# The low part of relu in two of eight token groups: from one VectorE instruction to a ScalarE and a GpSimd instruction

## The chip, the cores and the metric

The kernel runs on one core of a Trainium2 chip. The metric is device microseconds of one execution. The engines are TensorE (PE: matmuls; PEld: its weight loads), VectorE (DVE), ScalarE (ACT), GpSimd (POOL) and SyncE (SP), whose queue issues the DMAs used here. Each engine executes its own list of instructions in a fixed order and waits on semaphores for the others.

## What is computed

Three stages follow each other: a recurrence over 768 tokens (32 batch-heads of width 40), a feed-forward block with a norm, and a second feed-forward block with a three-tap convolution and a gate. Only the second stage is touched by the change:

```python
xn = (x - mu) / np.sqrt(var + 1e-06) * g_ln
ch = np.maximum(xn @ w_ch1, 0.0) @ w_ch2
return (x + ch).astype(np.float32)
```

`x` has 4 x 768 rows of 320; `w_ch1` is 320 x 1280, `w_ch2` is 1280 x 320. The weights arrive as float64.

## The kernel before

The first half of the program (to about 490 us) is the recurrence. Then come eight groups of 384 tokens (TG). Each goes through `ffn` (the first block, ten column blocks f = 0..9 of 128 hidden units) and `hidden` (the second block's up-product, eight blocks, results in the tile `h`), while convolution, gate and down-product of finished pieces run as tasks beside them.

**Two parts for every number.** Products are made in a rounded format (FP32R), and precision is kept by splitting each operand into a high part (the rounded value) and a low part (value minus high part). Three matmul passes (high x high, high x low, low x high) replace one. So the relu between the two products is also needed in two parts, `rh` and `rl`. `relu_parts` (lines 973 to 979) makes `rh` on ScalarE from the PSUM tile `ups` (L977) and `rl = max(ups, 0) - rh` on VectorE in one instruction, again from PSUM (L978).

**The work of one block f.** TensorE makes `ups` with 8 matmuls (L960, `up`) and adds the block into three PSUM tiles `acc` with 9 matmuls (L970, `down`): six that read `rh`, three that read `rl`. `ffn` calls `up` one block ahead of `down`. There are two PSUM buffers for `ups` and three buffers each of `rh` and `rl`. After block 9, VectorE adds `acc` to `x` (L995), which frees the three PSUM tiles for the next transposes (`tps`, L938).

**Weights are converted beside the first two groups.** In groups 0 and 1, and in the `hidden` blocks that follow, the float64 weights still come in. One conversion (`Weights.load`, `value`, `step`) is: a DMA into one of four buffers (`raw`, twice, and two halves of `o`; L792); ScalarE squares the high words into `q` (L803); VectorE builds the float32 value `v` in four dependent instructions (L804, L805, L807, L810); ScalarE rounds it to the high part, for instance `w4h` (L818, CAST); GpSimd subtracts for the low part, `w4l` (L820). There are two buffers of `v`. From the start of group 0 there are 6 conversions left for w2 (128x320), 12 for w3 (128x256), 8 for w4 (128x320) and one small one for the convolution's taps.

**Order.** The order of each engine's list is not written by hand: the program is emitted in the order of `first`, `ffn` and `hidden`, and a list scheduler with its own timing model then sorts the instructions of each engine. On the chip the order is fixed. Of importance here: an instruction of ScalarE that waits for a conversion (L818) holds up the relus behind it.

Of the kernel before, what the change touches and what calls it, by code (L numbers as in the profile page):

```python
# [10 lines left out]
AF = mybir.ActivationFunctionType  # L11
ALU = mybir.AluOpType
# [718 lines left out]
N1, N2 = F1 // 128, F2 // 128  # L731
TG = 384
# [98 lines left out]
class Mlp:  # L831
# [138 lines left out]
                self.mm = self.nc.tensor.matmul(acc[n][:, 0:DM], lhsT=l, rhs=r, start=(f == 0 and i == 0),  # L970
                                                stop=(f == nf - 1 and i == 2)).ins

    def relu_parts(self, ps):
        nc = self.nc
        rh = self.pr.tile([128, TG], F32R, tag="rh", name="rh")
        rl = self.pr.tile([128, TG], F32R, tag="rl", name="rl")
        nc.scalar.activation(rh, ps, AF.Relu)  # L977
        nc.vector.scalar_tensor_tensor(out=rl, in0=ps, scalar=0.0, in1=rh, op0=ALU.max, op1=ALU.subtract)  # L978
        return rh, rl

    def ffn(self, g, xt, mid):

        nc = self.nc
        acc = [self.psa.tile([128, 512], F32, tag="a", name="acc") for _ in range(NT)]
        self.ws.until(1)
        parts = self.relu_parts(self.up(self.w1h, self.w1l, 0, xt))
        for f in range(N1):
            self.ws.until(f + 2)
            nxt = self.relu_parts(self.up(self.w1h, self.w1l, f + 1, xt)) if f + 1 < N1 else None
            self.down(acc, parts, self.w2h, self.w2l, f, N1)  # L990
            parts = nxt
            mid(f)
        x = self.x2[g]
        for n in range(NT):
            nc.vector.tensor_tensor(out=x[:, n], in0=acc[n][:, 0:DM], in1=x[:, n], op=ALU.add)  # L995
        return x
# [295 lines left out]
```

## Time and profile before

| | us |
|---|---|
| median of 3 runs | 933.29 (930.16 to 936.09) |
| the profiled execution | 932.86 |
| its span, first to last instruction | 931.1 |

| engine | busy, us | share of the span |
|---|---|---|
| PE | 810.3 | 87% |
| DVE | 650.7 | 70% |
| ACT | 511.7 | 55% |
| POOL | 297.5 | 32% |

The shares are averages over very different stages. In the page's forty slices TensorE is at 8 to 9 tenths from 490 us on, VectorE at 9 from about 490 to 610 us and far lower later, and GpSimd does little after 570 us. What a change in groups 0 and 1 is worth must be read from about 498 to 590 us.

### The profile page before, as it was taken

The numbers are of one execution on the slowest core, as the hardware profiler recorded it, in microseconds if no ns is written. First come the engines' busy times: TensorE is split into PE (matmuls) and PEld (weight loads), VectorE is DVE, ScalarE is ACT, GpSimd is POOL, SyncE is SP. The second block draws the span as 40 slices with busy tenths as digits, with TensorE's granted clock in tenths as the row PEclk, the third lists the DMA queues.
The fourth block names the chain that finished last, engine by engine and source line by source line (L and its number), as shares of the span: only waits on it lengthen the run. The fifth ranks groups of instructions, "written<-read, shape, count | busy, mean of one in ns | idle before, by whom it ended". The sixth has DMA issues, their size and how long they took to land.

```text
span 931.1 us, 24745 instructions
## 1 busy us (share of the span) xinstructions
PE 810.3 (87%) x9911; PEld 714.8 (77%) x9911; DVE 650.7 (70%) x1528; ACT 511.7 (55%) x1166; POOL 297.5 (32%) x519
## 2 busy tenths in 40 slices
PE   1655579899879989979788898999999999999995
PEld 1444368667657767767667797999999999999994
DVE  8859757666656855787898999957368563847264
ACT  6257448677558656556454346836256353727263
POOL 9415269368359276086112222000000000000014
PEclk9766679999999989989899899999999999999998
DMA  6994696667687774773746341001010100000000
GB/s 165 202 239 122 184 211 135 153 130 186 160 170 175 180 149 123 137 158 85 176 120 171 86 128 48 15 1 36 1 50 1 36 1 15 15 1 29 1 15 32
DMA packets 218543, 94.20 MB, mean 101 GB/s; under 512 B 176860, under 2 KB 207924, under 8 KB 218420
## 3 DMA queue, kind: packets, MB, share of 16 engines
q1 hardware_dynamic: 217524, 90.24, 40.9%
q0 software_dynamic: 896, 2.30, 1.2%
q8 instruction: 80, 1.31, 0.6%
q14 instruction: 43, 0.35, 0.1%
HBM read 63.78 MB, written 28.72 MB: 99 GB/s over the span
## 4 chain that ended last, share of the span: by engine, by line
PE 45%; DVE 23%; DMA 10%; ACT 7%; SPq 5%; issue 4%; POOL 4%; DVEq 0%; ACTq 0%; POOLq 0%
PE ups L960 17%; PE acc L970 8%; PE accb L970 8%; DVE r L495 5%; PE reps L478 2%; PE tps L938 2%; SPq L448 2%; SPq L217 2%; PE aps L396 2%; DMA raw<-in_moe_w_ch_dram 2%; PE tr L322 2%; DVE l L414 2%; ACT yt L134 2%; PE xrps L547 1%; DMA ld_w<-in_w_dram 1%
## 5 line engine op out<-in xcount | busy, mean ns | idle before, releaser
L1024 POOL TENSOR_TENSOR pl<-c,ph 128x512 fp32r<-128x512 f32 x8 | 13.5, 1708 | 334.2 <-ACT ph L1021 334.2
L978 DVE SCALAR_TENSOR_TENSOR rl<-ups,rh 128x384 fp32r<-128x384 f32 x80 | 44.2, 554 | 83.0 <-ACT rh L977 82.9
L977 ACT ACTIVATE rh<-ups 128x384 fp32r<-128x384 f32 x80 | 38.9, 488 | 101.8 <-PE ups L960 101.6
L495 DVE TENSOR_TENSOR r<-zhps,zmask 32x576 f32<-32x576 f32 x96 | 72.0, 750 | 25.8 <-PE zhps L491 24.0
L435 POOL TENSOR_TENSOR sv<-sv,svt 128x30 f32<-128x30 f32 (+9 forms) x150 | 80.9, 539 | 10.0
L433 POOL TENSOR_TENSOR svt<-sv 128x30 f32<-128x30 f32 (+9 forms) x150 | 78.7, 525 | 9.6
L960 PE MATMUL ups<-xh,w1h 128*128 128x384 f32 x240 | 81.5, 342 | 0.0
L960 PE MATMUL ups<-xh,w1l 128*128 128x384 f32 x240 | 81.0, 337 | 0.0
L970 PE MATMUL acc<-w2h,rh 128*128 128x320 f32 x240 | 71.6, 310 | 1.6 <-ACT rh L977 1.6
L508 PE MATMUL xps<-r,l 128*40 128x72 f32 x1536 | 61.8, 238 | 11.1 <-issue 6.7
L970 PE MATMUL acc<-w2l,rh 128*128 128x320 f32 x240 | 71.4, 307 | 0.0
L508 PEld LDWEIGHTS xps<-r,l 128*40 128x40 f32 x1536 | 54.6, 124 | 18.0 <-issue 8.9
L960 PE MATMUL ups<-xh,w3h 128*128 128x384 f32 x192 | 64.3, 339 | 2.0 <-ACT h L1002 2.0
L134 ACT COPY yt<-xps 40x256 f32<-40x256 f32 x96 | 35.2, 367 | 55.5 <-DVE r L519 52.4
L960 PE MATMUL ups<-xh,w3l 128*128 128x384 f32 x192 | 64.6, 336 | 0.0
L414 DVE TENSOR_TENSOR l<-aps,mask 32x256 f32<-32x256 f32 x96 | 40.0, 417 | 29.4 <-ACT pst L401 28.2
L970 PE MATMUL accb<-w4h,ph 128*128 128x320 f32 x192 | 59.0, 314 | 1.2 <-ACT ph L1021 1.2
L970 PE MATMUL accb<-w4l,ph 128*128 128x320 f32 x192 | 58.6, 308 | 0.0
L960 PE MATMUL ups<-xl,w1h 128*128 128x384 f32 x160 | 54.2, 339 | 0.4 <-DVE xl L944 0.4
L1013 DVE SCALAR_TENSOR_TENSOR c<-h,taps,c 128x256 f32<-128x256 f32 (+1 forms) x88 | 45.7, 528 | 12.6 <-ACT c L1011 12.4
L970 PE MATMUL accb<-w4h,pl 128*128 128x320 f32 x192 | 53.4, 311 | 0.8 <-POOL pl L1024 0.7
L519 DVE TENSOR_TENSOR r<-xps,ge 40x320 f32<-40x320 f32 x96 | 46.8, 488 | 9.4 <-PE xps L508 8.0
(190 smaller groups left out, 2278.6 us busy)
## 6 DMA issues: line engine op xcount, KB each, us to landing
l<-ks SPq DMA_DIRECT2D x44, 160.0 KB, 3.6
raw<-in_moe_w_ch_dram SPq DMA_DIRECT2D x17, 320.0 KB, 3.4
ks<-p_b SPq DMA_DIRECT2D x12, 416.0 KB, 3.3
ks<-p_k SPq DMA_DIRECT2D x12, 416.0 KB, 4.3
ld_w<-in_w_dram SPq DMA_DIRECT2D x24, 160.0 KB, 3.4
ld_k<-in_k_dram SPq DMA_DIRECT2D x24, 160.0 KB, 4.4
ld_a<-in_a_dram SPq DMA_DIRECT2D x24, 160.0 KB, 3.4
ld_b<-in_b_dram SPq DMA_DIRECT2D x24, 160.0 KB, 4.4
```

The lines of the kernel that those rows point to most:

```text
L134: return self.nc.scalar.copy(out, in_).ins
L414: nc.vector.tensor_tensor(out=lv[v0:v0 + C, :, :, y, c, 32 * half:32 * half + C], in0=pv[64 * y:64 * y + C, :, :, half], in1=self.mask[64 ...
L433: eng.tensor_tensor(out=tmp, in0=sv[:, 0:u, u:u + 1].to_broadcast([128, u, m]), in1=sv[:, u:u + 1, u + 1:C].to_broadcast([128, u, m]), op= ...
L435: last = eng.tensor_tensor(out=sv[:, 0:u, u + 1:C], in0=sv[:, 0:u, u + 1:C], in1=tmp, op=ALU.add)
L495: nc.vector.tensor_tensor(out=r1[z0:z0 + 32, :, :, MO[y]:MO[y] + 72], in0=ps[32 * y:32 * y + 32], in1=self.zmask[32 * y:32 * y + 32].rearr ...
L508: nc.tensor.matmul(ps[x0:x0 + D, j >> 2, o:o + 72], lhsT=l2[:, i, :], rhs=r1[:, j, MO[y]:MO[y] + 72], start=True, stop=True)
L519: last = nc.vector.tensor_tensor(out=r2[X0:X0 + D, :, :, VO[y]:VO[y] + D], in0=pv[x0:x0 + D, :, :, v:v + D], in1=ge[X0:X0 + D, :, :, y, c: ...
L960: self.mm = self.nc.tensor.matmul(ps, lhsT=l, rhs=r, start=(i == 0), stop=(i == len(passes) - 1)).ins
L970: self.mm = self.nc.tensor.matmul(acc[n][:, 0:DM], lhsT=l, rhs=r, start=(f == 0 and i == 0), stop=(f == nf - 1 and i == 2)).ins
L977: nc.scalar.activation(rh, ps, AF.Relu)
L978: nc.vector.scalar_tensor_tensor(out=rl, in0=ps, scalar=0.0, in1=rh, op0=ALU.max, op1=ALU.subtract)
L1013: nc.vector.scalar_tensor_tensor(out=c, in0=h(1), scalar=w(1), in1=c, op0=ALU.mult, op1=ALU.add)
```

## The change

In groups 0 and 1 (`g < 2`) `relu_parts` gets a scratch tile `r`, a slice of the tile `h` that `hidden` fills later. ScalarE then makes relu twice from the same PSUM tile, once rounded into `rh` and once in full into `r` (L979 of the changed kernel), and GpSimd subtracts, `rl = r - rh` (L980). Groups 2 to 7 keep the VectorE instruction (now L982). Lines below are six higher than before from there on, so L995 becomes L1001 and L1002 becomes L1008.

```diff
-    def relu_parts(self, ps):
+    def relu_parts(self, ps, r=None):
         nc = self.nc
         rh = self.pr.tile([128, TG], F32R, tag="rh", name="rh")
         rl = self.pr.tile([128, TG], F32R, tag="rl", name="rl")
         nc.scalar.activation(rh, ps, AF.Relu)
-        nc.vector.scalar_tensor_tensor(out=rl, in0=ps, scalar=0.0, in1=rh, op0=ALU.max, op1=ALU.subtract)
+        if r is not None:
+            nc.scalar.activation(r, ps, AF.Relu)
+            nc.gpsimd.tensor_tensor(out=rl, in0=r, in1=rh, op=ALU.subtract)
+        else:
+            nc.vector.scalar_tensor_tensor(out=rl, in0=ps, scalar=0.0, in1=rh, op0=ALU.max, op1=ALU.subtract)
         return rh, rl
 
     def ffn(self, g, xt, mid):
...
+        r = lambda f: self.h[:, f % N2, 1:TG + 1] if g < 2 else None
         self.ws.until(1)
-        parts = self.relu_parts(self.up(self.w1h, self.w1l, 0, xt))
+        parts = self.relu_parts(self.up(self.w1h, self.w1l, 0, xt), r(0))
         for f in range(N1):
             self.ws.until(f + 2)
-            nxt = self.relu_parts(self.up(self.w1h, self.w1l, f + 1, xt)) if f + 1 < N1 else None
+            nxt = self.relu_parts(self.up(self.w1h, self.w1l, f + 1, xt), r(f + 1)) if f + 1 < N1 else None
```

The scheduler sorts the whole stage anew. Three places matter.

ScalarE, end of group 1, before: `rh_8322` is block 8 of the group, `rh_8355` block 9; each CAST is the end of one w4 conversion.

```order
L818 CAST w4h_7579<-v_8271 128x320
L803 ACTIVATE q_8336<-o_7653 128x320
L977 ACTIVATE rh_8258<-ups_8249 128x384
L818 CAST w4h_7579<-v_8303 128x320
L803 ACTIVATE q_8369<-raw_8344 128x320
L977 ACTIVATE rh_8290<-ups_8281 128x384
L818 CAST w4h_7579<-v_8335 128x320
L803 ACTIVATE q_8389<-raw_8377 128x320
L977 ACTIVATE rh_8322<-ups_8313 128x384
L818 CAST w4h_7579<-v_8368 128x320
L803 ACTIVATE q_8434<-o_7653 128x320
L977 ACTIVATE rh_8355<-ups_8346 128x384
```

The same place of the changed kernel, from the third w4 CAST on: `rh_8307` is block 7, `rh_8340` block 8, `rh_8374` block 9, and the rows `h_7584<-ups` the second relus.

```order
L818 CAST w4h_7579<-v_8354 128x320
L803 ACTIVATE q_8409<-raw_8397 128x320
L977 ACTIVATE rh_8307<-ups_8298 128x384
L979 ACTIVATE h_7584<-ups_8298 128x384
L818 CAST w4h_7579<-v_8388 128x320
L803 ACTIVATE q_8454<-o_7653 128x320
L818 CAST w4h_7579<-v_8408 128x320
L803 ACTIVATE q_8474<-o_7653 128x320
L977 ACTIVATE rh_8340<-ups_8331 128x384
L979 ACTIVATE h_7584<-ups_8331 128x384
L818 CAST w4h_7579<-v_8453 128x320
```

Block 8's relu stood behind the third w4 CAST and now stands behind the fifth; block 9's moved from behind the fourth to behind the sixth.

GpSimd, same place, changed kernel (before, the eight w4l rows follow each other with nothing between):

```order
L820 TENSOR_TENSOR w4l_7580<-v_8354,w4h_7579 128x320
L980 TENSOR_TENSOR rl_8308<-h_7584,rh_8307 128x384
L820 TENSOR_TENSOR w4l_7580<-v_8388,w4h_7579 128x320
L820 TENSOR_TENSOR w4l_7580<-v_8408,w4h_7579 128x320
L980 TENSOR_TENSOR rl_8341<-h_7584,rh_8340 128x384
L820 TENSOR_TENSOR w4l_7580<-v_8453,w4h_7579 128x320
L980 TENSOR_TENSOR rl_8375<-h_7584,rh_8374 128x384
```

Each low part now waits its turn behind the low parts of the weights.

TensorE, end of group 1 in the changed kernel, from the last matmuls of block 9's `up` on (`w1`), through block 8's six `rh` matmuls, whose rows begin here:

```order
L970 MATMUL acc<-w2h,rl 128x320 x3
L970 MATMUL acc<-w2h,rh 128x320
L970 MATMUL acc<-w2l,rh 128x320
L970 MATMUL acc<-w2h,rh 128x320
L970 MATMUL acc<-w2l,rh 128x320
L970 MATMUL acc<-w2h,rh 128x320
L970 MATMUL acc<-w2l,rh 128x320
L960 MATMUL ups<-xh,w3h 128x384
```

These are block 8's `rl` and block 9's `rh`; the first of the `hidden` blocks (8 matmuls with w3) stands ahead of them and the second behind, then block 9's `rl`. Before, block 8's `rl` followed its `rh` at once. A low part is thus wanted one block of matmuls later than before.

## Rows read from the trace of the kernel before

**Rows 1.** Busy by stretch: PE, PEld, DVE, ACT, POOL; then PEclk, DMA, GB/s
```profile
498.00:525.00 27.00, 25.05 (x156) 24.14 (x157) 24.80 (x85) 11.28 (x28) 7.82 (x8) 1.00 0.62 166
525.00:529.60 4.60, 1.35 (x9) 0.83 (x7) 4.60 (x19) 0.74 (x2) 1.03 (x1) 0.88 0.35 94
529.60:537.70 8.10, 7.85 (x35) 6.52 (x35) 7.97 (x20) 4.81 (x12) 1.47 (x2) 0.65 0.14 44
590.00:870.00 280.00, 278.92 (x1775) 277.07 (x1774) 177.57 (x468) 143.96 (x361) 0.00 (x0) 1.00 0.05 17
```
**Rows 2.** PE's waits, 498 to 600 us: in total, times, longest
```profile
PE acc L970 <- DVE rl L978: 3.1, 5, 1.6
PE ups L960 <- ACT h L1002: 2.0, 4, 1.2
PE tps L938 <- DVE x L995: 1.7, 1, 1.7
```
**Rows 3.** DVE by line and form, 500 to 566 us: count, busy us, mean ns
```profile
L978 DVE SCALAR_TENSOR_TENSOR rl<-ups,rh 128x384 fp32r<-128x384 f32 x20 | 10.8, 546 | 0.2 <-ACT rh L977 0.2
L810 DVE SCALAR_TENSOR_TENSOR v<-q,v 128x320 f32<-128x320 bf16 x10 | 6.0, 598 | 0.1
...
L922 DVE SCALAR_TENSOR_TENSOR y<-t,y 128x3 f32<-128x3 f32 x12 | 3.8, 315 | 0.0
L805 DVE SCALAR_TENSOR_TENSOR v<-raw,v 128x320 int32<-128x320 int32 x5 | 3.0, 603 | 0.0
...
L920 DVE SCALAR_TENSOR_TENSOR t<-y 128x3 f32<-128x3 f32 x12 | 2.8, 234 | 0.0
...
L921 DVE TENSOR_TENSOR t<-t,v 128x3 f32<-128x3 f32 x12 | 1.8, 149 | 0.0
```
**Rows 4.** DVE in order of time, 559 to 566 us: start, us
```profile
559.43 1.06 DVE L810 SCALAR_TENSOR_TENSOR v<-q,v 128x320 f32<-128x320 bf16 x1
560.41 0.55 DVE L978 SCALAR_TENSOR_TENSOR rl<-ups,rh 128x384 fp32r<-128x384 f32 x1
560.88 0.31 DVE L804 TENSOR_SCALAR v<-raw 128x320 int32<-128x320 int32 x1
561.22 1.07 DVE L805 SCALAR_TENSOR_TENSOR v<-raw,v 128x320 int32<-128x320 int32 x1
...
562.97 0.48 DVE L810 SCALAR_TENSOR_TENSOR v<-q,v 128x320 f32<-128x320 bf16 x1
```
**Rows 5.** POOL in order of time, from 559 us
```profile
559.03 1.10 POOL L820 TENSOR_TENSOR w4l<-v,w4h 128x320 fp32r<-128x320 f32 x1 [2.55 <-ACT w4h L818]
```
**Rows 6.** POOL by line and form, 490 to 566 us
```profile
L820 POOL TENSOR_TENSOR w3l<-v,w3h 128x256 fp32r<-128x256 f32 x12 | 10.2, 848 | 28.5 <-ACT w3h L818 28.4
L820 POOL TENSOR_TENSOR w2l<-v,w2h 128x320 fp32r<-128x320 f32 x6 | 6.1, 1027 | 15.8 <-ACT w2h L818 15.8
L820 POOL TENSOR_TENSOR w4l<-v,w4h 128x320 fp32r<-128x320 f32 x5 | 4.9, 983 | 8.6 <-ACT w4h L818 8.6
```
**Rows 7.** ACT in order of time, 558 to 566 us: third, fifth, sixth w4 cast
```profile
558.50 0.46 ACT L818 CAST w4h<-v 128x320 fp32r<-128x320 f32 x1 [2.20 <-DVE v L810]
...
559.27 0.47 ACT L977 ACTIVATE rh<-ups 128x384 fp32r<-128x384 f32 x1
...
563.49 0.46 ACT L818 CAST w4h<-v 128x320 fp32r<-128x320 f32 x1 [1.72 <-DVE v L810]
...
565.81 0.46 ACT L818 CAST w4h<-v 128x320 fp32r<-128x320 f32 x1 [1.47 <-DVE v L810]
```
**Rows 8.** PE in order of time, 560 to 565 us: block 8, last of block 9, hidden
```profile
560.19 0.30 PE L970 MATMUL acc<-w2h,rh 128*128 128x320 f32 x1
...
561.55 0.34 PE L960 MATMUL ups<-xh,w3h 128*128 128x384 f32 x1
...
564.38 0.71 PE L970 MATMUL acc<-w2h,rl 128*128 128x320 f32 x3 [0.37 <-DVE rl L978]
564.92 0.34 PE L960 MATMUL ups<-xh,w3h 128*128 128x384 f32 x1
```

## Prediction

> **What bounds the kernel now.** I read the busy times by stretch first [rows 1]. From 590 to 870 us TensorE is busy 278.92 of 280 us at full clock: whatever it is early or late by at 590 us goes straight into the end. So the change is worth what it does to TensorE between 498 and 590 us. There VectorE is the crowded engine: 24.80 of 27 us between 498 and 525 us, 4.60 of 4.60 us in the next stretch [rows 1]. ScalarE (11.28 of 27) and GpSimd (7.82 of 27) have room.
>
> The waits of TensorE come next [rows 2]. It lost 3.1 us for `rl` (L978) and 1.7 us for the sums of x (L995), both ended by VectorE, and 2.0 us for ScalarE's `h` in the `hidden` blocks. The gap at 525 to 529.6 us, where it was busy 1.35 us, is followed by 8.1 us at a mean granted clock of 0.65 (so part at 1.2, part at 2.4 GHz); that is 8.1 x 0.35 = 2.8 us more [rows 1]. All that VectorE costs TensorE here is therefore 3.1 + 1.7 + 2.8 = 7.6 us, and no relief of VectorE alone brings more.
>
> **What the change removes.** Twenty `rl` instructions of 0.546 us leave VectorE [rows 3]. They overlap their successors a little: from the start of one at 560.41 to the next instruction at 560.88 are 0.47 us [rows 4]. So 20 x 0.47 = 9.4 us of VectorE's time go, and the 3.1 us of waits for L978 with them, if nothing takes their place.
>
> **What it adds on ScalarE.** Twenty second relus. I cost them like the first ones, 0.47 us as at 559.27 [rows 7], 9.4 us in all. They lie in ScalarE's idle time (15.7 us idle of 27 between 498 and 525 us [rows 1]), and the next block's matmuls hide the later release of the PSUM buffer: one block of `hidden` matmuls and the three passes of `down` beside it are over 2 us (561.55 to 564.38 [rows 8]). Without that cover each would cost 0.47 us. I take nothing.
>
> **What it adds on GpSimd.** Twenty subtractions of 128x384. The trace has the same form, two SBUF inputs and a rounded output, at 128x256 (0.848 us) and 128x320 (0.983 to 1.027 us) [rows 6]. From 0.848 and 0.983, 0.135 us per 64 columns, my estimate at 384 is 1.12 us. With one weight subtraction per block, GpSimd needs 1.0 + 1.1 = 2.1 us, and TensorE needs 564.92 - 561.55 - 0.37 = 3.0 us for one up-product and one `down` [rows 8]. That fits. The order also wants each low part one block of matmuls later than before, so waits for `rl` should vanish. I take nothing for GpSimd's own length.
>
> **The toll on VectorE.** This is the term that decides. At 559.43 L810 takes 1.06 us; at 562.97 the same instruction takes 0.48 us [rows 4]. The long one coincides with a GpSimd subtraction that runs from 559.03 for 1.10 us [rows 5], and the L805 at 561.22 (1.07 us) looks the same. The `rl` at 560.41 is not stretched: its 0.55 us is the mean of all twenty [rows 3, 4]. So a GpSimd subtraction holds up VectorE instructions, and the one instruction that the change removes is of a kind that it does not hold up. One toll is 1.06 - 0.48 = 0.58 us. A lower bound is the mean: over L810 (10 x (0.598 - 0.48)), L805 (5 x (0.603 - 0.48)), L922 (12 x (0.315 - 0.149)) and L920 (12 x (0.234 - 0.149), the 0.149 from L921) VectorE lost 1.2 + 0.6 + 2.0 + 1.0 = 4.8 us [rows 3]. Spread over 23 subtractions [rows 6] that is 0.21 us each, with the other forms left out. An upper bound is the subtraction's whole length, 1.12 us. I take a toll of L = 0.5 us: nearer to the single 0.58, since no `rl` is left on VectorE to fill the time, less a little for norm instructions that might. Then twenty tolls are 10 us against 9.4 us saved: VectorE is not relieved at all.
>
> The Trainium skill (SBUF — State Buffer, section "Who interferes with whom") says that a VectorE instruction with two SBUF inputs and a GpSimd instruction that reads SBUF share a read interface, and that the second to start waits for the whole of the first; one with a single SBUF input goes through. The trace agrees on which instructions are stretched (L810, not `rl`), but the stretch of 0.58 us is shorter than the GpSimd instruction's 1.10 us. By that rule taken at its word the toll would be the whole 1.12 us, which is the last rival below.
>
> **What moves on ScalarE.** The scheduler placed the relus as if VectorE had become faster. Block 8's relu in group 1 stood behind the third w4 CAST and now stands behind the fifth; block 9's behind the sixth instead of the fourth. ScalarE runs in order, so these relus wait for VectorE's conversions, and TensorE waits for them, with the last of group 1 and the `hidden` blocks queued behind.
>
> Where is the fifth CAST? At 563.49 before [rows 7]. Ahead of its L810 in VectorE's list 19 `rl` and one L804 (about 0.2 us) are gone: 19 x 0.47 + 0.2 = 9.1 us; otherwise the list holds the same instructions up to there. Eighteen GpSimd subtractions are new: 18 L. With L = 0.5 the CAST comes 9.0 - 9.1 = -0.1 us off, at 563.4. From CAST to end of relu takes (559.27 + 0.47) - 558.50 = 1.24 us in the same sequence CAST, square, relu [rows 7], so the relu ends at 564.6 and TensorE can start at about 564.7. Before, it started block 8's `down` at 560.19 [rows 8]. **That is 4.5 us later.**
>
> Block 9's relu waits for the sixth CAST, at 565.81 before, again shifted by about nothing, and ends at 567.0. TensorE comes to it after six matmuls, a `hidden` block and three matmuls, 0.9 + 1.4 + 0.45 us after 564.7, at 567.5: no second wait. Block 8's `rl` follows the fifth w4l: 564.0 + 1.0 + 1.1 = 566.1, wanted at 567.0, so it is covered by 0.9 us and costs the excess if GpSimd is slower. The 0.37 us wait for `rl` at 564.38 [rows 8] goes.
>
> Group 0 has the same pattern, one conversion instead of two, and the sums of x come when VectorE comes to them. Whatever is won or lost there up to 4 us does not count: TensorE would wait at the fifth CAST for the rest.
>
> **Sum.** +4.5 - 0.37 = +4.1 us at 565 us. Of the 2.0 us waits for `h` [rows 2], which hang on ScalarE and VectorE and come at the same time while TensorE comes later, I give back two thirds, -1.3 us (an estimate). Net +2.8 us on the profiled execution's 932.86: 935.7. The median shown (933.29) is 0.4 us above that execution, so I predict 936.0.
>
> **Rivals.**
> *Tie.* The toll is about 0.3 us, near the mean. The fifth CAST comes 18 x 0.3 - 9.1 = -3.7 us earlier, the wait shrinks from 4.5 to 0.8 us, less 0.37 and part of the 1.3: 932 to 933. For it: the mean. Against: the mean includes subtractions that met an `rl`.
> *Gain.* The toll is below 0.26 us (18 L - 9.1 = -4.5, where the wait is gone). Then VectorE's waits go too, at most 7.6 us: 925. For it: GpSimd instructions may fall on norm work or idle time. Against: VectorE idles hardly at all.
> *Slower.* VectorE stands still for the subtraction's whole 1.12 us. The fifth CAST moves by 18 x 1.12 - 9.1 = +11.1 us; 11.1 + 4.1 - 1.3 = +13.9, so 947. It passes +1% (9.3 us) from L = 0.87 on. For it: the subtraction is longer than any of the stretch, and a crowded VectorE always has a two-input instruction ready. Against: 0.58 us at 1.10 us length.
>
> **How the numbers follow.** Forecast (L from 0.38 to 0.7; 933.5 to 939.5): 0.50. Tie: 0.20. Gain (924 to 930): 0.15. Slower (940 to 947): 0.15. The range leaves out the better half of the gain and most of the slow case: 927 to 943. About 1%, 9.3 us, is what a measurement can tell from no change. Faster by more than that needs more than the 7.6 us of VectorE's waits: 0.04. Slower by more: 0.11. Within: 0.85.
>
> **What would show it.** In the changed kernel's profile: L805, L807 and L810 stretched about twice as often; VectorE as busy from 498 to 566 us as before although twenty instructions are gone; a TensorE wait of about 4 us ended by ScalarE's `rh` just before the first `hidden` block, with the w4 CAST ahead of it waiting for L810; no waits for `rl` beyond 1 us. The prediction is wrong if the fifth w4 CAST comes before 560 us or after 570 us, if TensorE waits for GpSimd's `rl` instead, or if the `hidden` waits swallow the whole delay.

## The result, and the profile after

The changed kernel takes 939.24 us in the median (933.73 to 949.3, 12 runs), the kernel before 935.77 us (927.99 to 944.89) on the same chip: a ratio of 1.0063, 95% interval [1.0036, 1.009]. (The medians are over all 12 runs; this ratio and those below compare the fast runs alone, so it is not the quotient of the two medians, 1.0037.) It is 0.6% slower, within 1%; 936.0 had been predicted, and the time lies within 927 to 943. The profiled execution has 937.71 us, with a span of 936.0 us.

The busy time by stretch, columns as in [rows 1]:

```profile
498.00:525.00 27.00, 23.09 (x143) 22.29 (x144) 24.50 (x72) 13.03 (x35) 15.63 (x17) 1.00 0.60 154
525.00:529.60 4.60, 2.98 (x19) 2.37 (x17) 4.60 (x16) 1.50 (x4) 2.79 (x3) 1.00 0.25 57
529.60:537.70 8.10, 5.26 (x22) 4.71 (x23) 7.85 (x23) 3.71 (x8) 1.60 (x2) 0.61 0.26 75
590.00:870.00 280.00, 278.92 (x1774) 277.07 (x1774) 183.40 (x490) 148.59 (x375) 0.00 (x0) 1.00 0.05 17
```

From 590 us on nothing has changed (278.92 of 280 us in both). VectorE is as full as before between 498 and 525 us (24.50 against 24.80 us), although instructions have left it, and TensorE has lost 2 us there (23.09 against 25.05). What TensorE waits for, 498 to 600 us (in total, times, longest):

```profile
PE acc L970 <- ACT rh L977: 11.3, 11, 2.5
PE tps L938 <- DVE x L1001: 2.8, 1, 2.8
PE ups L960 <- ACT h L1008: 1.7, 4, 0.8
PE acc L970 <- POOL rl L980: 0.2, 1, 0.2
```

The 3.1 us for VectorE's `rl` [rows 2] have gone, and for GpSimd's `rl` it hardly waits. In their place stand 11.3 us for ScalarE's `rh`, the first relu, which the change left on its engine. The longest, 2.47 us, is the one that the prediction named: block 8 of group 1. ScalarE's and TensorE's rows, in order of time (start, us):

```profile
565.88 0.46 ACT L818 CAST w4h<-v 128x320 fp32r<-128x320 f32 x1 [1.59 <-DVE v L810]
566.25 0.48 ACT L803 ACTIVATE q<-o 128x320 bf16<-128x320 f32 x1
566.64 0.47 ACT L977 ACTIVATE rh<-ups 128x384 fp32r<-128x384 f32 x1
...
569.18 0.46 ACT L818 CAST w4h<-v 128x320 fp32r<-128x320 f32 x1 [1.69 <-DVE v L810]
```

```profile
567.16 0.41 PE L970 MATMUL acc<-w2h,rh 128*128 128x320 f32 x1 [2.47 <-ACT rh L977]
```

The fifth w4 CAST waits for VectorE's L810, the relu stands behind it, and block 8's `down` starts at 567.16 instead of 560.19 us [rows 8]. VectorE by line and form, 500 to 566 us (count, busy us, mean ns), and GpSimd's new line, 490 to 566 us:

```profile
L810 DVE SCALAR_TENSOR_TENSOR v<-q,v 128x320 f32<-128x320 bf16 x9 | 5.5, 615 | 0.4
L921 DVE TENSOR_TENSOR t<-t,v 128x3 f32<-128x3 f32 x12 | 4.8, 400 | 0.0
...
L807 DVE SCALAR_TENSOR_TENSOR v<-raw,v 128x320 int32<-128x320 int32 x5 | 4.1, 819 | 0.1
...
L805 DVE SCALAR_TENSOR_TENSOR v<-raw,v 128x320 int32<-128x320 int32 x5 | 3.3, 655 | 0.1
```

```profile
L980 POOL TENSOR_TENSOR rl<-h,rh 128x384 fp32r<-128x384 f32 x18 | 18.7, 1046 | 5.8 <-ACT h L979 3.3 <-POOL w3l L820 2.1 <-POOL w4l L820 0.2
```

L921, on 128x3, takes 0.400 us in the mean in place of 0.149 [rows 3], and L922 and L920 rose too; L807 in this form went from 0.487 to 0.819; L805 in this form only from 0.603 to 0.655 and L810 from 0.598 to 0.615 [rows 3], but L810 on 128x256 rose from 0.432 to 0.541. L807's row in the kernel before, then L810's on 128x256 before and after:

```profile
L807 DVE SCALAR_TENSOR_TENSOR v<-raw,v 128x320 int32<-128x320 int32 x5 | 2.4, 487 | 0.1
L810 DVE SCALAR_TENSOR_TENSOR v<-q,v 128x256 f32<-128x256 bf16 x12 | 5.2, 432 | 0.0
```

```profile
L810 DVE SCALAR_TENSOR_TENSOR v<-q,v 128x256 f32<-128x256 bf16 x12 | 6.5, 541 | 0.2
```

Counted over all forms of the conversions and the norm, from the start of the stage to the sixth w4 CAST: in the kernel before 17 VectorE instructions took over 0.15 us longer than their form does undisturbed, 8.7 us in all, and in the changed one 34, 21.1 us in all. What left VectorE as `rl` came back as stretched instructions.

**A ruler for what follows.** The stage begins with GpSimd's memset of `h` (L875), in the kernel before and in the changed one at

```profile
490.54 0.11 POOL L875 MEMSET h<- 128x8 f32 x1 [3.76 <-PE xps L508]
```

```profile
489.21 0.11 POOL L875 MEMSET h<- 128x8 f32 x1 [3.77 <-PE xps L508]
```

Counted from there the sixth w4 CAST, which has the same VectorE instructions ahead of it in nearly all kernels here (`rl` aside, and the runs of v_late8, v_late8a and v_l6, which move conversions), came at 565.81 - 490.54 = 75.3 us [rows 7], and after the change at 569.18 - 489.21 = 80.0: VectorE is 4.7 us later, not relieved. From the memset to the end of the span it was 931.07 - 490.54 = 440.5 us and is 936.01 - 489.21 = 446.8: +6.3. To TensorE's last matmul it was 431.8 us and is 439.5: +7.7.

### The profile page after: what moved, and what is told of

It is laid out like the page before. It is cut to its first block, busy times and chain, and to the rows that moved or that the text cites. A ratio compares the mean times of both kernels' runs of the same rounds, so it can differ in the third digit from the quotient of the medians.

```text
span 936.0 us, 24805 instructions
## 1 busy us (share of the span) xinstructions
PE 809.6 (86%) x9911; PEld 714.7 (76%) x9911; DVE 657.2 (70%) x1508; ACT 519.3 (55%) x1186; POOL 318.2 (34%) x539
## 4 chain that ended last, share of the span: by engine, by line
PE 45%; DVE 23%; DMA 8%; ACT 8%; SPq 6%; POOL 5%; issue 5%; DVEq 0%; POOLq 0%; ACTq 0%
PE ups L960 16%; PE acc L970 8%; PE accb L970 8%; DVE r L495 4%; SPq L448 2%; DMA ld_w<-in_w_dram 2%; PE tps L938 2%; DVE p_k L286 2%; PE aps L396 2%; PE tr L322 2%; PE reps L478 2%; ACT yt L134 2%; DVE l L414 2%; POOL sv L435 2%; ACT l L134 1%
## 5 line engine op out<-in xcount | busy, mean ns | idle before, releaser
L982 DVE SCALAR_TENSOR_TENSOR rl<-ups,rh 128x384 fp32r<-128x384 f32 x60 | 33.4, 556 | 81.3 <-ACT rh L977 81.0
L970 PE MATMUL acc<-w2h,rh 128*128 128x320 f32 x240 | 72.5, 313 | 11.3 <-ACT rh L977 11.3
L970 PEld LDWEIGHTS acc<-w2h,rh 128*128 128x128 f32 x240 | 45.1, 188 | 14.3 <-ACT rh L977 14.3
L519 DVE TENSOR_TENSOR r<-xps,ge 40x320 f32<-40x320 f32 x96 | 46.8, 487 | 10.3 <-PE xps L508 8.9
```

The costliest lines, as they stand in the source:

```text
L519: last = nc.vector.tensor_tensor(out=r2[X0:X0 + D, :, :, VO[y]:VO[y] + D], in0=pv[x0:x0 + D, :, :, v:v + D], in1=ge[X0:X0 + D, :, :, y, c: ...
```

## The experiments

The theory by then: each GpSimd subtraction holds VectorE up by more than the `rl` that it saves, so VectorE's conversions come later, and the order on ScalarE makes TensorE wait for them. Rivals: the order alone; the toll alone; the second relus or GpSimd's own length.

A scheduler orders each program anew, and an edit that removes a cost also moves instructions. So in the runs whose label begins with p_ the order is held: the instructions' names stand in the kernel as a list for each engine, and each is chained behind the one ahead of it there, without a wait:

```
for i in row:                      # one engine's list, in the order wanted
    if last is not None:
        tc.add_manual_dep(i, last.name, mybir.DependencyInfo(
            mybir.DependencyClass.NoSync, mybir.DependencyReason.DATA), reason="pin")
    last = i
```

The times, each against the kernel before on the same chip, and marks of the profiled execution, in us later (+) than in the kernel before, all counted from that execution's memset of `h`:

| run | ratio, 95% interval | group 0's first relu | group 0's sums of x | sixth w4 CAST | block 8's relu, group 1 | group 1's sums | TensorE's last matmul | end of the span |
|---|---|---|---|---|---|---|---|---|
| the change | 1.0063 [1.0036, 1.0090] | +0.4 | +4.8 | +4.7 | +8.7 | +9.6 | +7.7 | +6.3 |
| p_memset | 0.9900 [0.9849, 0.9951] | +0.1 | -0.6 | -7.0 | -2.2 | -2.7 | -4.3 | -5.8 |
| p_toll | 1.0074 [1.0041, 1.0106] | +0.8 | +5.6 | +9.1 | +8.5 | +9.1 | +9.1 | +7.7 |
| p_half | 1.0029 [0.9992, 1.0066] | -0.3 | +0.9 | +2.5 | +2.3 | +2.5 | +2.5 | +1.1 |
| p_relu2 | 1.0021 [0.9987, 1.0055] | -0.1 | -0.3 | -0.5 | -0.5 | -0.5 | -0.6 | -1.7 |
| p_moved | 1.0031 [1.0000, 1.0062] | 0.0 | -0.3 | -0.1 | +3.9 | +1.6 | +2.5 | +1.7 |
| p_oldorder | 1.0036 [0.9998, 1.0073] | +1.5 | +3.2 | +6.0 | +5.4 | +6.0 | +6.0 | +4.8 |
| p_oldact | 1.0098 [1.0063, 1.0133] | -0.2 | +4.2 | +5.1 | +3.8 | +9.3 | +9.3 | +8.1 |
| e_g0 | 1.0015 [0.9979, 1.0051] | +1.3 | +5.1 | +2.8 | +4.7 | +5.1 | +5.0 | +3.6 |
| v_late8 | 0.9976 [0.9946, 1.0006] | +1.0 | +1.0 | +10.1 | +0.4 | -2.3 | +0.6 | -0.4 |
| v_late8a | 1.0061 [1.0024, 1.0097] | +0.1 | +4.5 | +15.9 | +3.6 | +3.2 | +5.3 | +4.1 |
| v_hand | 1.0022 [0.9987, 1.0057] | -0.3 | -2.7 | +0.1 | +0.1 | +0.1 | +0.1 | -0.6 |
| v_l6 | 0.9972 [0.9939, 1.0005] | +0.9 | -2.2 | +10.3 | -2.0 | -5.8 | +0.3 | -0.4 |

The marks tell more than the times: the stage began anywhere from 486.3 (p_toll) to 500.8 us (v_late8) in these executions, ahead of everything that the edits touch, and that scatter is in every total. Two things scatter in the marks as well. Group 0's first relu stands in ScalarE's list behind an instruction that waits for a weight's DMA, and it came 0.3 us earlier to 1.5 us later than in the kernel before; no edit adds or removes an instruction ahead of it, so differences of about 1 us between marks show nothing by themselves. And the end of the span includes the last DMA to the output: from TensorE's last matmul to the end it was 8.7 us in the kernel before and 7.3 to 8.0 us in all the others, so that the end makes each of them look 0.7 to 1.4 us better than it is. TensorE's last matmul is the better mark.

**Is it the toll? p_memset.** In the changed kernel, order held:

```
-            nc.gpsimd.tensor_tensor(out=rl, in0=r, in1=rh, op=ALU.subtract)
+            nc.gpsimd.memset(rl.bitcast(F32), 0.0)
```

> The changed kernel with its order of instructions held on every engine; GpSimd writes zeros into rl (a memset, which reads nothing) in place of the subtraction, so the low part of relu is left out in groups 0 and 1. Theory (VectorE pays a toll for each GpSimd subtraction, and only that lateness makes the new order of ScalarE cost anything): the toll of about 0.7 us x 20 is gone, the 9.4 us of rl stay saved, the fifth w4 CAST comes near 555 us instead of 565.9, TensorE's waits for rh fall from 11.3 us to under 3 us, and the time is 3 to 7 us below the kernel before (ratio 0.992 to 0.997). Rival (the order alone costs it, whatever GpSimd reads): the relus stand behind the same casts as in the changed kernel, so the time stays 4 to 7 us above (1.004 to 1.008). Rival (the second relu on ScalarE costs it): also unchanged, 1.004 to 1.008.

GpSimd's memset by line and form, and TensorE's waits, 498 to 600 us:

```profile
L980 POOL MEMSET rl<- 128x384 f32 x20 | 8.1, 417 | 0.2 <-PE acc L970 0.2
```

```profile
PE tps L938 <- DVE x L1001: 2.9, 1, 2.9
PE acc L970 <- ACT rh L977: 2.4, 3, 1.5
PE ups L960 <- ACT h L1008: 1.3, 3, 0.7
```

The same relus behind the same casts, the same second relus, and the waits for `rh` fall from 11.3 to 2.4 us; the sixth CAST comes 11.7 us earlier than in the changed kernel (4.7 + 7.0), and the time is 1% below the kernel before, a little more than expected. So the order and the second relu cost nothing that shows when VectorE is this early, and 11.7 / 19 = 0.62 us is what a subtraction costs VectorE more than a memset (19 of the twenty stand ahead of that CAST). The memset differs in two things, it reads nothing and is shorter (0.417 against 1.046 us). The rows part them. GpSimd's and VectorE's in p_memset:

```profile
540.86 0.42 POOL L980 MEMSET rl<- 128x384 f32 x1 [0.21 <-PE acc L970]
```

```profile
540.88 0.39 DVE L805 SCALAR_TENSOR_TENSOR v<-o,v 128x256 int32<-128x256 int32 x1
```

This L805 begins with 0.40 us of the memset left and keeps its usual time, and so do an L807 (0.414 us) and an L810 (0.411 us) that begin with 0.34 us left: these instructions, with two SBUF inputs, are held up by a GpSimd instruction that reads, not by one that only writes. That TensorE waited for GpSimd's length itself is excluded by the 0.2 us of waits for it in the changed kernel. VectorE wins 7.0 us, not the 9.4 of the removed `rl`: 0.8 us went to more stretching (9.5 us in all against 8.7; L921 has 0.289 us here in place of 0.149), 0.6 us to more idle time, and what is left over says that each `rl` was worth 0.42 us and not 0.47.

**The toll alone, and its size: p_toll, p_half.** In the kernel before, order held, a subtraction that nobody reads; p_half does it on half the columns:

```
         nc.scalar.activation(rh, ps, AF.Relu)
+        if r is not None:
+            nc.gpsimd.tensor_tensor(out=r, in0=rh, in1=rh, op=ALU.subtract)
```

> The kernel before, its order held on every engine, with twenty GpSimd subtractions of 128x384 added (rh minus rh into the idle tile h, read by nobody); rl stays on VectorE. Theory: L810 320 rises from about 0.60 to about 0.68 us in the mean and L805, L807 likewise, VectorE is 8 to 13 us later by the third w4 CAST, and the time is 5 to 10 us above the kernel before (1.005 to 1.011). Rival (GpSimd does not hold VectorE up): within 1 us (0.999 to 1.001).

> As p_toll (the kernel before, its order held, twenty GpSimd subtractions added that nobody reads), with half the columns: 128x192 in place of 128x384. If the toll goes by how long GpSimd's subtraction runs, less a fixed overlap, the sixth w4 CAST comes 3 to 5 us after that of the kernel before (counted from the stage's start) in place of p_toll's 9.1, and the time is 2 to 4 us above (1.002 to 1.0045). Rival (a fixed toll for each instruction): 9 us at the CAST and 1.007 as in p_toll.

GpSimd's line in p_toll and in p_half, and TensorE's longest wait in p_toll:

```profile
L979 POOL TENSOR_TENSOR h<-rh 128x384 f32<-128x384 f32 x20 | 18.4, 925 | 9.2 <-ACT rh L977 9.2
```

```profile
L979 POOL TENSOR_TENSOR h<-rh 128x192 f32<-128x192 f32 x20 | 12.3, 621 | 8.9 <-ACT rh L977 8.9
```

```profile
PE acc L970 <- DVE rl L980: 8.2, 11, 2.2
```

Twenty subtractions that nobody needs, on an engine that has room, make the kernel 0.74% slower. Each puts the sixth CAST off by 9.1 / 20 = 0.46 us with `rl` still on VectorE. With the subtraction 0.30 us shorter (0.621 for 0.925 us) it is 2.5 / 20 = 0.13 us, below the 3 to 5 us in all that I had expected. Part of that is VectorE's idle time, which is 1.9 us less in p_half than in the kernel before. Read off the stretched instructions themselves, the added subtractions cost 8.6 us in p_toll and 3.5 us in p_half, 0.43 and 0.18 us each: the toll falls about as much as the subtraction does. A fixed toll for each instruction is excluded. (p_half's ratio alone, 1.0029, can't be told from 1.)

**The second relu: p_relu2.** The kernel before, order held, and only this added:

```
+        if r is not None:
+            nc.scalar.activation(r, ps, AF.Relu)
```

> The kernel before, its order held on every engine, with the second relu of groups 0 and 1 added on ScalarE right behind the first; rl stays on VectorE, and nobody reads what the second relu writes. Theory: 9.4 us more work on ScalarE in its idle time, so within 1.5 us of the kernel before (0.998 to 1.002). Rival (ScalarE's relus cost the time): 3 us or more above (1.003 and over).

Every mark up to TensorE's last matmul lies 0.1 to 0.6 us ahead of the kernel before and TensorE's waits for `rl` are the same 3.1 us. The ratio's interval holds 1. The second relu is free to what can be measured.

**The moved relus alone: p_moved.** The kernel before, order held but for blocks 8 and 9 of group 1 (ScalarE's list; `rl` moves with them on VectorE):

```
 L818 CAST w4h<-v 128x320
 L803 ACTIVATE q<-raw 128x320
-L977 ACTIVATE rh<-ups 128x384
 L818 CAST w4h<-v 128x320
 L803 ACTIVATE q<-o 128x320
-L977 ACTIVATE rh<-ups 128x384
 L818 CAST w4h<-v 128x320
 L803 ACTIVATE q<-o 128x320
-L818 CAST w4h<-v 128x320
+L977 ACTIVATE rh<-ups 128x384
+L818 CAST w4h<-v 128x320
+L977 ACTIVATE rh<-ups 128x384
```

> The kernel before, its order held on every engine, except that the relus of blocks 8 and 9 in group 1 stand behind the fifth and sixth w4 CAST as in the changed kernel (their rl behind the same conversions on VectorE). No instruction is added or removed: it measures the moved order alone. By the prediction's step block 8's down starts 4 to 5 us later and 2.5 to 4 us of it reach the end (1.0025 to 1.0045). Rival (VectorE's list alone decides): within 1 us (0.999 to 1.001).

```profile
PE acc L970 <- ACT rh L977: 5.1, 3, 3.4
...
PE ups L960 <- ACT h L1002: 1.1, 2, 0.7
```

Above, TensorE's waits in p_moved, 498 to 600 us. Nothing is added, VectorE is on time (sixth CAST -0.1), block 8's relu comes 3.9 us later, and the waits for `h` shrink from 2.0 to 1.1. Of the delay 2.5 us reach TensorE's last matmul in the profiled execution, and 0.31% (2.9 us) the times, whose interval just touches 1. The step of the prediction agrees with that: the order costs about this much if VectorE is neither helped nor hurt.

**The order undone: p_oldorder, p_oldact.** p_oldorder has the changed kernel's work in the order of the kernel before on all engines. p_oldact has the changed kernel's order, except that the relu pairs that had got behind one or two more casts go back to their old places on ScalarE, and GpSimd's subtractions with them. These are eleven pairs; as relus read alike in the list, three places in it change, not five as the expectation says.

The end of group 1 in ScalarE's list, where the last two pairs of the changed kernel stood behind the fifth and sixth w4 CAST and the last now stands behind the fourth:

```
 L818 CAST w4h<-v 128x320
 L803 ACTIVATE q<-o 128x320
+L977 ACTIVATE rh<-ups 128x384
+L979 ACTIVATE h<-ups 128x384
 L818 CAST w4h<-v 128x320
 L803 ACTIVATE q<-o 128x320
-L977 ACTIVATE rh<-ups 128x384
-L979 ACTIVATE h<-ups 128x384
 L818 CAST w4h<-v 128x320
 L803 ACTIVATE q<-raw 128x320
-L977 ACTIVATE rh<-ups 128x384
-L979 ACTIVATE h<-ups 128x384
```

> The work of the changed kernel in the order of the kernel before on all engines: its VectorE list less the twenty rl, its TensorE list, its ScalarE list with each second relu behind the first, GpSimd's rl behind the conversion that goes ahead of it. Theory by now (VectorE's list decides how long the stage is, the order of ScalarE does not): the sixth w4 CAST comes 4 to 6 us later after the stage's start than in the kernel before, as in the changed kernel, and the time is 4 to 9 us above the kernel before (1.004 to 1.010), part of it new waits for GpSimd's rl. Rival (the prediction's step: the relus behind two more casts cost it): 0 to 2 us above (1.000 to 1.002).

> The changed kernel with its order held on every engine, except that the five relu pairs of groups 0 and 1 that had moved behind one or two more casts stand again where the kernel before has them in ScalarE's list (GpSimd's subtractions move with them). Theory (toll and order together): VectorE stays as late as in the changed kernel, but block 8's relu waits for the third w4 CAST only; TensorE's waits for rh fall from 11.3 us to under 6 us, the wait ahead of block 8 from 2.5 us to under 1 us, and the time is 0 to 2.5 us above the kernel before (1.000 to 1.003). Rival (the toll alone): the time stays 4 to 7 us above (1.004 to 1.008). Rival (the order alone): same as the kernel before or up to 3 us below (0.997 to 1.000).

TensorE's waits, 498 to 600 us, in p_oldorder and then in p_oldact:

```profile
PE acc L970 <- ACT rh L977: 3.8, 4, 2.8
PE tps L938 <- DVE x L1001: 3.8, 2, 3.6
PE ups L960 <- ACT h L1008: 2.8, 4, 1.2
PE acc L970 <- POOL rl L980: 1.3, 4, 0.5
```

```profile
PE tps L938 <- DVE x L1001: 6.2, 1, 6.2
PE ups L960 <- ACT h L1008: 5.6, 4, 4.3
PE acc L970 <- ACT rh L977: 3.3, 4, 1.3
```

In the old order the sixth CAST is 6.0 us late and so is TensorE's last matmul: the toll without the moved relus, with 1.3 us of waits for GpSimd's `rl` in it, and with the 1.5 us by which its first relu was late before any subtraction ran. Less those 1.5 us and with p_moved's 2.5 that makes 7.0; the change, less the 0.4 us of its own first relu, has 7.3: the two add up within the scatter. This rests on the marks. The ratio, 1.0036, lies just below the 1.004 to 1.010 that I had expected, and its interval holds 1 and the rival's 1.000 to 1.002. p_oldact I had expected 0 to 2.5 us above the kernel before, and it is the slowest of all. Its relus are early (the waits for `rh` fall to 3.3 us), but VectorE's list is still that of the changed kernel, where group 1's sums stand behind all eight w4 conversions and that of the taps:

```profile
578.16 0.78 DVE L810 SCALAR_TENSOR_TENSOR v<-q,v 24x128 f32<-24x128 bf16 x1
578.87 1.27 DVE L1001 TENSOR_TENSOR x<-acc,x 128x320 f32<-128x320 f32 x3
```

The sums start at 578.87 - 492.53 = 86.3 us, as in the changed kernel (86.6). TensorE, early now, waits for VectorE elsewhere: 6.2 us for the sums of group 0, 4.3 us for an `h` that stands behind casts. The waits taken away on ScalarE came back on other engines, since VectorE's list behind them had not become shorter. Beyond that, the 4.3 us wait for `h` (it ended at 575.99 us) was followed by a stretch at the lower of TensorE's two clock levels, 1.2 of 2.4 GHz (columns as in [rows 1], a granted clock of 0.50):

```profile
575.33:582.16 6.83, 6.17 (x21) 6.07 (x22) 4.50 (x10) 2.44 (x7) 1.85 (x2) 0.50 0.00 0
```

The kernel before and the changed kernel have one such stretch of 6.8 us in these two groups, p_oldact has two. The second is worth at most 6.8 x 0.5 = 3.4 us, which covers the 1.7 us by which p_oldact's last matmul comes behind that of the changed kernel.

**Where in the program: e_g0, v_late8, v_late8a.** e_g0 is the change in group 0 alone, in the scheduler's order (`if g < 1` in place of `if g < 2`). v_late8 is the kernel before with VectorE's conversions of five w4 blocks put behind group 1's sums; v_late8a is that edit in the changed kernel:

```
-        x = self.ffn(1, xt1, lambda f: ws.step(NM))
+        x = self.ffn(1, xt1, lambda f: ws.step(NM) if f < 8 else None)
...
             self.hidden(0, f, xt2[0])
-            ws.step(NM)
+            with self.order(last):            # last: the last sum of x of group 1
+                ws.step(NM)
```

> The change in group 0 alone (ten second relus and ten GpSimd subtractions; group 1's rl stay on VectorE), in the scheduler's own order. By the prediction's step that group 0 does not count up to 4 us: within 1 us of the kernel before (0.999 to 1.001). By the theory that VectorE's lateness in group 0 goes through to the end (its sums of x came 4.8 us later in the changed kernel): 2 to 4.5 us above (1.002 to 1.005).

> The kernel before, with VectorE's conversions of the last five w4 blocks queued behind the sums of x of group 1 (they are needed only by the products after that). No work is left out. If VectorE's list is what holds TensorE between 498 and 590 us, the sums come 8 to 12 us earlier on VectorE, TensorE's waits for rl and h in group 1 go, and the time is 2 to 6 us below the kernel before (0.993 to 0.998). Rival (the conversions collide with the hidden blocks instead: ScalarE's h behind CASTs that wait for VectorE): 0 to 5 us above (1.000 to 1.005).

> The changed kernel with the same edit (VectorE's conversions of the last five w4 blocks behind the sums of x of group 1). If the change costs time only because VectorE is crowded, most of its 6 us go away with the crowding in group 1 and what is left is group 0's part: within 3 us of the kernel before (0.997 to 1.003) and 1 to 4 us above the same edit without the change. Rival (GpSimd's way to rl or the second relu costs TensorE directly): still 4 to 7 us above the same edit without the change.

Group 0 alone puts its sums off by 5.1 us and the last matmul by 5.0, of which 1.3 us were there at the first relu, before any subtraction ran. Its ratio of 1.0015 can't be told from 1, nor from 1.004. v_late8 brought group 1's sums 2.3 us forward on VectorE, not the 8 to 12 that I had expected. With group 1 uncrowded the change still costs 5.3 - 0.6 = 4.7 us at the last matmul, where I had expected 1 to 4 us to be left, and its ratio (1.0061) lies above that of v_late8 (0.9976) by more than either interval's half width. By the marks, then, about half of the loss or more is made in group 0 and not at block 8 of group 1. The times of e_g0 (0.15%, 1.4 us) neither show nor exclude it.

**A faster version? v_hand, v_l6.** v_hand is the kernel before with VectorE's list written by hand at the gap of 525 us: group 0's last `rl` and its sums go ahead of seven conversion instructions (and block 4's `rl` up by five places). VectorE's list there, before and then after that edit:

```
L921 L805 L920 L922 L804 L807 L921 L920 L805 L810 L922 L978 L921 L807 L927 x3 L922 L995 L810 L995 x2
L978 L921 L920 L922 L921 L920 L922 L921 L927 x3 L922 L995 x3 L805 L804 L807 L805 L810 L807 L810
```

v_l6 puts conversions behind the sums of both groups, by the edit of v_late8 and this one:

```
-            ws.step(NM)                       # in group 0's mid
+            if f < 6:
+                ws.step(NM)
...
-        x = self.ffn(1, xt1, lambda f: ws.step(NM))
+        x = self.ffn(1, xt1, mid1)            # mid1: ws.step(NM) behind group 0's last sum
```

> The kernel before, order held on every engine, with two places of VectorE's list written by hand: rl of group 0's block 9 and the three sums of x go ahead of seven conversion instructions that stood between them (their CASTs on ScalarE behind the three xh), and rl of block 4 goes up by five places. No work is left out. If the gap of TensorE at 525 to 530 us (1.57 us for rl, 1.68 us for the sums) and the low clock behind it come from VectorE's order alone, 2 to 5 us go: 0.9945 to 0.998. Rival (the conversions, later by 2 us, hold up what follows by as much): 0.999 to 1.001.

> The kernel before with the conversions spread: VectorE's part of them waits behind group 0's sums of x from the seventh step of group 0 on (some w3 blocks go from group 0 to group 1), and behind group 1's sums for seven of the eight w4 blocks. No work is left out. If VectorE's list between 498 and 566 us is what holds TensorE, both sums come earlier, the gap at 525 to 530 us and the low clock behind it go, and the time is 2 to 6 us below the kernel before (0.9935 to 0.998). Rival (the conversions put off collide with the hidden blocks and the convolution): 0.999 or more.

```profile
PE tps L938 <- DVE xl L944: 3.9, 1, 3.9
...
PE acc L970 <- DVE rl L978: 0.8, 3, 0.4
```

Above, v_hand's waits: those for `rl` fall from 3.1 to 0.8 us, the sums come 2.7 us earlier, and TensorE then waits 3.9 us for `xl`, the next thing that VectorE owes it. Every mark from there on is back at +0.1; the rival expectation (0.999 to 1.001) was the better one. v_l6 brings group 1's sums 5.8 us forward and gives it back behind them (last matmul +0.3). Its ratio of 0.9972 and v_late8's 0.9976 are below 1, with intervals that hold 1: no version is shown to beat the kernel before. p_memset shows what there would be to win (about 1%, interval 0.5 to 1.5%) if `rl` cost VectorE nothing.

## Why the prediction was right, point by point

- **What bounds the kernel**: right. TensorE is full from 590 us on in both, and what it is late by there is the result.
- **No relief for VectorE**: right, and shown by p_memset and p_toll. The busy time from 498 to 525 us is almost the same with the instructions gone.
- **The size of the toll, L = 0.5 us**: too low, and the term that was mis-sized. The fifth CAST, counted from the stage's start, was at 563.49 - 490.54 = 72.95 and is at 565.88 - 489.21 = 76.67: +3.7 where the formula gave -0.1. From 18 L - 9.1 = 3.7 follows L = 0.71, with all that the formula leaves out in it. Read off the stretched instructions up to the sixth CAST, the toll is (21.1 - 8.7) / 19 = 0.65 us, and p_memset against the change gives 0.62; the rest is that an `rl` gone freed 0.42 us and not the 0.47 of the prediction (which goes with p_memset too), and that VectorE idled 0.7 us more. The weight subtractions are not the rest: they stretched 17 instructions before and 17 after, by 8.7 and 9.0 us. The prediction's lower bound of 0.21 was too low as well: it summed four forms (4.8 us), and the same trace has 8.7 us over all forms, 0.38 for each of 23 subtractions. With L = 0.71 its sum is 4.1 + 3.7 - 1.3 = 6.5, against 6.3 us at the end of the span and 7.7 at TensorE's last matmul.
- **The moved relus, +4.5 us at block 8, +2.8 at the end**: right in mechanism and in size, by p_moved (3.9 at block 8; 2.5 at the last matmul, 2.9 in the times). But the prediction had this as the whole cost and the toll as a draw. The marks show it as the smaller part: 2.5 of 7.7 at the last matmul, and the toll 4.5 to 6.0 (p_oldorder, without and with its late first relu).
- **Group 0 does not count up to 4 us**: wrong. The reasoning was that TensorE would wait at the fifth CAST anyway. But VectorE is late by 4.8 us already at group 0's sums, its list is full from there on, and by the marks of e_g0 and v_late8a the lateness is not swallowed. It did the sum no harm, since the formula for the fifth CAST counts group 0's subtractions with the rest; that was luck.
- **The second relu and GpSimd's length at nothing**: right (p_relu2; 0.2 us of waits for GpSimd's `rl`). The estimate of 1.12 us for the subtraction measured 1.05 in the mean, with waits of its own in it: the shortest took 0.86.
- **1.3 us given back of the waits for `h`**: 0.3 was (2.0 to 1.7); p_moved gave back 0.9.
- **One wait of about 4 us ahead of the first hidden block**: it is 2.47 us there, with ten smaller ones for `rh` before it. L805, L807 and L810 are stretched more than twice as often, as expected (by over 0.15 us, up to the sixth CAST: 6 before, 16 after, over all their forms); the 128x3 instructions of the norm (L921) took much of the rest, which the prediction had counted on to make the toll smaller.
- The rival *slower* set its mark at L = 0.87 for +1%. At 0.71 the formula gives 6.5 of those 9.3 us, and the time stayed below the mark (0.63%).
- **The size as a whole**: the forecast was +2.7 us, and the ratio says +5.9. The time, 939.24, is still within the 933.5 to 939.5 of the forecast case, by 0.3 us; the L that goes with it, 0.71, is just outside the 0.38 to 0.7 that the case was given. So the range held by its width more than by the sum.

So each part of the mechanism was right, their weights were not, and the time came out 3 us above the forecast mainly by one term: a toll of 0.65 to 0.71 us for 0.5.

## What to carry to other kernels

Work moved from a full VectorE to an idle GpSimd is not free for VectorE: in this stage a subtraction of 1.05 us cost it about 0.65 us, more than the 0.42 us that it saved. What decides is which instruction leaves and what stays: the one moved here read PSUM and was of the kind that GpSimd doesn't disturb, and most of what stayed is of the other kind. And where one engine's list is full, count how late it is at a mark that all variants share: waits on the other engines move about (p_oldact, v_hand) and their sum says little. Look first at how far such a mark scatters where no edit acts.

## What the runs showed of the hardware

How the toll works can be read from two pairs of rows of the changed kernel, GpSimd's and VectorE's:

```profile
552.58 1.01 POOL L980 TENSOR_TENSOR rl<-h,rh 128x384 fp32r<-128x384 f32 x1 [0.30 <-POOL w3l L820]
```

```profile
552.63 0.97 DVE L922 SCALAR_TENSOR_TENSOR y<-t,y 128x3 f32<-128x3 f32 x1
```

The subtraction ends at 553.59, the 128x3 instruction at 553.60; this instruction takes 0.15 us elsewhere. The other pair:

```profile
547.08 0.99 POOL L980 TENSOR_TENSOR rl<-h,rh 128x384 fp32r<-128x384 f32 x1 [0.40 <-POOL w3l L820]
```

```profile
547.26 0.83 DVE L915 TENSOR_SCALAR v<-mv 128x3 f32<-128x3 f32 x1
```

These end at 548.07 and 548.09, and this VectorE instruction has one input. So a VectorE instruction of these kinds that begins inside a GpSimd subtraction waits for its end, however small it is itself. The whole changed kernel says it with more rows. Of the VectorE instructions between 497 and 585 us that began with over 0.14 us of a GpSimd subtraction left, these ended so long after it:

| VectorE instruction | number | ended after the subtraction, us | its own time elsewhere, us |
|---|---|---|---|
| two SBUF inputs, 128x320 (L805, L807, L810) | 12 | 0.347 to 0.352 | 0.48 to 0.49 |
| two SBUF inputs, 128x256 (the same lines) | 7 | 0.279 to 0.284 | 0.41 to 0.42 |
| two SBUF inputs, 128x3 (L920, L921, L922) | 12 | 0.016 to 0.024 | 0.15 |
| TENSOR_SCALAR, one SBUF input, 128x320 (L804) | 2 | 0.185 to 0.186 | 0.32 |
| the same, 128x256 | 2 | 0.150 to 0.155 | 0.28 |

In every row that is 0.13 to 0.14 us less than the instruction's own time, so the stretch is what is left of the subtraction less about 0.13 us; those that began in the last 0.06 us of one kept their own time, and so did the sums of x (0.476 us with 0.73 us left) and L909 (0.476 us with 0.57 us left). It works the other way round too, at GpSimd's cost: in the kernel before an L807 that began 0.03 us after a w3l subtraction by the trace (521.86 us) took its usual 0.41 us, and the subtraction 1.04 us, where five others of its form took 0.73 to 0.76. An `rl`, with one input in PSUM, does not wait. In p_toll, GpSimd's and VectorE's rows:

```profile
564.37 1.08 POOL L979 TENSOR_TENSOR h<-rh 128x384 f32<-128x384 f32 x1
```

```profile
564.69 0.55 DVE L980 SCALAR_TENSOR_TENSOR rl<-ups,rh 128x384 fp32r<-128x384 f32 x1
```

It begins 0.32 us into the subtraction, is done at 565.24, before that ends at 565.45, and has its usual 0.55 us. The toll is what is left of the subtraction when the next instruction of the other kind begins, less 0.13 us: it grows with the subtraction's length (p_toll, p_half), and an `rl` in between can run through a part of it. The prediction had read the 0.58 us stretch of L810 beside 1.10 us as a toll of half the length. It was the rest: the subtraction of 559.03 [rows 5] ended at 560.13, 0.70 us after L810 began at 559.43 [rows 4], and 0.70 less 0.13 is 0.57. And the `rl` of 560.41, which it gave as one that runs through, began after that end; its row proved nothing, though the conclusion holds.

The Trainium skill (SBUF — State Buffer, section "Who interferes with whom") states this: the first to issue has the shared interface for its whole instruction, the other is blocked; VectorE's two-SBUF-input instructions meet GpSimd's reads, and `tensor_scalar` meets GpSimd too when it runs in a two-port mode. The rows agree with it. So does p_memset, where GpSimd only writes: its L805, L807 and L810 ran through, while one L804, a `tensor_scalar`, was held up beside a memset too (0.50 us, ending 0.18 us behind it). The prediction set the rule at its word equal to a toll of the whole length, and the rows show it is the rest of the length. It also gave the rule as if every instruction with a single SBUF input went through; the Trainium skill excepts the two-port modes there, and the rows have L804 and L915, each with a single SBUF input, held up. No run here shows which mode those two ran in.
